# A reserve of MLP work after row 0, and a new interleaving of old steps with token steps, in a threshold-attention and MLP-mixer kernel

## The chip, the cores and the metric

The kernel runs on one core of one Trainium2 chip. The metric is the device time of one execution in microseconds (us); the number of a kernel is the median of several executions. A profiled execution gives the time of each instruction on each engine: PE (TensorE, matrix multiplication; its weight loads are listed apart as PEld), DVE (VectorE), ACT (ScalarE), POOL (GpSimd) and SP (SyncE, which here issues DMA transfers).

## The reference

Eight batch rows, eight heads, 576 positions, head dimension 64. The first block is attention with a threshold under the maximum; the second is a mixer MLP, along the positions (token MLP) and then along the features (channel MLP). The MLP weights come as 64-bit floats.

```python
scores = scale * np.matmul(q, k.transpose(0, 1, 3, 2))
thresh = np.max(scores, axis=-1, keepdims=True) - tau
scores = np.where(scores >= thresh, scores, -1000000000.0)
scores = scores - np.max(scores, axis=-1, keepdims=True)
attn = np.exp(scores)
attn = attn / (np.sum(attn, axis=-1, keepdims=True) + 1e-09)
x = np.matmul(attn, v)                       # (8, 8, 576, 64)
x = x.transpose(0, 2, 1, 3).reshape(8, 576, 512)
...
h = np.maximum(xt @ w_tok1, 0.0) @ w_tok2    # xt: x with its last two axes exchanged; 576 -> 256 -> 576
u = x + h.transpose(0, 2, 1)
h2 = np.maximum(u @ w_ch1, 0.0) @ w_ch2      # 512 -> 1536 -> 512
return u + h2
```

## The kernel before, in words

**Units.** Attention runs in 144 units, 18 for each batch row (`UB`, line 87). A unit is up to 128 query positions of two heads against all 576 keys; of nine units, the fifth (`SHARED`) takes the last 64 positions of two head pairs. The loop at line 525 has one iteration for each unit u, and some more at the end. It issues instructions for all engines in an order written out by hand; every engine works through its own queue in that order.

**One iteration.** `scores(u)`: PE multiplies (line 301), DVE takes the maximum of each of two heads (306), POOL makes the bias (307). The two score tiles in PSUM are the only two, so the next scores wait until ACT has read these. `norm(u-1)`: DVE's reciprocal (325, 326) and POOL's scaling (329). In rows 1 and later then `weight(2)`; `turn_blocks(u-2)`: DVE turns 32x32 blocks (363), and when a group of two units is complete, sixteen DMAs on the SP queue move the blocks to their places in eT (373). Then `fill(0.4)`, `weight(2)`, `weigh(u)`: ACT's Prelu (316) and Exp (319); `fill(0.6)`, `weight(2)`, the loads of q and k on the ACT queue (106) and of v on SP (114), and `prep`, which turns q and k on DVE (283). Last, `values` (403, 408) two iterations after its group was turned: PE multiplies eT by v, ACT copies the result into xT (413). In row 0 the turning is done on PE instead (352, 354).

**Weights.** `weight` decodes 31 pieces of the MLP weights from 64-bit to 32-bit floats, three steps to a piece, on ACT (191, 193), DVE (201, 205, 209) and POOL (215). The load of a piece (176) is on the SP queue and goes into one of four raw buffers, so it waits for POOL's last step of the piece four before. Row 0 does two steps in an iteration; from iteration 18 there are six, two pieces, and the last piece is done in iteration 27.

**MLP steps and their plan.** When the last values of row b are issued, `push(b)` puts the row's MLP into the list `todo`, as steps with a cost in planner's microseconds. The token steps, from `token_mlp`: five `turn_x` (PE transposes x, line 425; ACT copies it, 426; cost 0.44), two `tok1` (434, relu on ACT 435; cost 4.3) and eight `tok2` (441, DVE adds to xT, 445; cost 0.97). Each kind needs all of the kind before: tok1 all five turns, tok2 both tok1. The channel steps, from `channel_mlp`, for groups of 256 positions: twelve `ch1` (463, relu on ACT 464; cost 1.72, or 0.86 for the half group) and for each 128 positions four `ch2` (475, 479; 3.0 or 2.6), the last with DVE's copy (484) and a store on SP (485). tok1, tok2, ch1 and ch2 share a pool of two PSUM buffers, `ps_mm`.

`push` interleaves the token steps with what is left in `todo` from the row before (`old`), one by one, then appends channel groups 0 and 1 of the pair of rows (b even) or 2 to 4 (b odd). Then it sets a quota: the sum of all costs less `KEEP` (45, but 0 after row 0), over 17. `fill(share)` takes steps from the front while a credit, raised by share x quota, is above 0. push(0) comes at the end of iteration 20, push(1) at the end of 39, and each later one 18 iterations further, push(b) at the end of 18 b + 21. Row 2's units start with iteration 36.

The names below: scores(u) for the scores of iteration u, tok1(0), tok1(1) for the two tok1, "share" for one of the two `fill` calls of an iteration.

Of the kernel before, what the change touches and what calls it, by code (L numbers as in the profile page):

```python
# [21 lines left out]
def kernel(  # L22
# [35 lines left out]
    NT = NI + 1  # L58
    MT = [P] * NI + [LAST]
    NP = H // 2  # L60
    NTK = DTOK // P
# [25 lines left out]
    UB = 9 * NP // 2  # L87
# [328 lines left out]
    def token_mlp(b):  # L416
        xT = xTs.pop(b)
        o = S * (b % 2)
        s = {}

        def turn_x(t):
            M = MT[t]
            ps = ps_tr.tile([P, MAIN], F32, tag="tr", name=f"tx_{b}_{t}").rearrange("p (c x) -> p c x", c=NP)
            for p in range(NP):
                nc.tensor.transpose(out=ps[0:M, p, :], in_=xT[:, p, o + t * P : o + t * P + M], identity=ident)  # L425
            nc.scalar.copy(out=x_sb[0:M, t, :], in_=ps[0:M].rearrange("q p d -> q (p d)"))

        def tok1(m):
            need(2)
            if m == 0:  # L430
                s["a"] = work.tile([P, NTK, DM], F32, tag="a", bufs=1, name=f"a_{b}")
            ps = ps_mm.tile([P, DM], F32, tag="mm", name=f"t1_{b}_{m}")
            for t in range(NT):
                nc.tensor.matmul(ps, lhsT=w1[:, t, P * m : P * m + P], rhs=x_sb[:, t, :], start=(t == 0), stop=(t == NT - 1))  # L434
            nc.scalar.activation(out=s["a"][:, m, :], in_=ps, func=AF.Relu)

        def tok2(c, f):
            need(6)
            ps = ps_mm.tile([P, HS], F32, tag="mm", name=f"t2_{b}_{c}_{f}")
            for m in range(NTK):  # L440
                nc.tensor.matmul(  # L441
                    ps, lhsT=s["a"][:, m, P * c : P * c + P], rhs=w2[:, m, HS * f : HS * f + HS], start=(m == 0), stop=(m == NTK - 1)
                )
            u = xT[:, c, o + HS * f : o + HS * f + HS]
            nc.vector.tensor_add(out=u, in0=u, in1=ps)  # L445

        steps = [(0.44, lambda t=t: turn_x(t)) for t in range(NT)]
        steps += [(4.3, lambda m=m: tok1(m)) for m in range(NTK)]
        steps += [(0.97, lambda c=c, f=f: tok2(c, f)) for c in range(NCC) for f in range(2)]
        return steps  # L450
# [41 lines left out]


    KEEP = 45.0
    todo = deque()
    quota = 0.0
    credit = 0.0
# [11 lines left out]
    def push(b):  # L509
        nonlocal quota  # L510
        uT = xTs[b]
        steps, old = token_mlp(b), list(todo)
        todo.clear()
        for i in range(max(len(steps), len(old))):
            todo.extend(old[i : i + 1])
            todo.extend(steps[i : i + 1])
        for i in range(2) if b % 2 == 0 else range(2, (2 * S + GR - 1) // GR):
            todo.extend(channel_mlp(b - b % 2, uT, i))
        quota = (sum(c for c, _ in todo) - (KEEP if b else 0.0)) / (UB - 1)

    prep(0)
    due = deque()
# [2 lines left out]
    for u in range(len(units) + LAG + 4):  # L525
# [4 lines left out]
        if on:  # L530
            b_now, p0, t = units[u]
            n = b_now * NP + p0
# [8 lines left out]
        if back:  # L541
# [6 lines left out]
            if place == many - 1:  # L548
                b, p, c = key
# [24 lines left out]
        while due and due[0][0] <= u:  # L574
            _, b, p, c = due.popleft()
            values(b, p, c)
            if p == NP - 1 and c == 1:
                push(b)
    need(len(pieces) - 1)
    quota = 1e9  # L580
# [29 lines left out]
```

## Time and profile before

| what | value |
|---|---|
| median of 3 executions | 1402.13 us (1402.13 to 1402.17) |
| profiled execution, its own time | 1403.98 us |
| its span, first to last instruction | 1401.9 us |
| mean granted clock of PE | 0.986 of full |
| DMA | 128.34 MB, mean 92 GB/s |

The profiled execution in 40 equal slices of 35 us, each digit the busy share of a slice in tenths, 9 for 90% or more; PEclk is the granted clock of PE, in tenths:

```profile
PE   5776899989999999999999999999999999999998
ACT  5676564444545444453334444443334444220110
PEclk9998999989999999999999999999999999999999
```

Row 0, without MLP work, takes the first slices; row 1 starts at about slice 4, row 2 at about slice 8. The PE rows below are from the timeline: start and length of a run of instructions of one line in us, engine, line, operation, tiles, shape and count, and in brackets the idle time of the engine before it and what ended it. The lengths of matmuls are modelled, so two runs may overlap a little.

### The profile page before, as it was taken

To read this page: it belongs to the slowest core of one execution; us is meant where nothing else is said; L and a number is where in the kernel's file an instruction comes from. 1 tells how busy PE (TensorE), PEld (TensorE's weight loads), DVE (VectorE), ACT (ScalarE), POOL (GpSimd) and SP (SyncE) were. 2 spreads that over 40 slices of the span, in tenths; PEclk is the share of its full clock that TensorE was granted. 3 is DMA by queue.
4 is the path that set the end of the run, shared out by engine and by line. 5 is a ranking of instruction groups with operands and counts; after the bars stand their busy time and mean duration, and the time that the engine had idled before them with its cause. 6 is when DMAs were issued, how large, how long until landed. Compare 5 with 4: busy or idle time off the path is not lost.

```text
span 1401.9 us, 19510 instructions
## 1 busy us (share of the span) xinstructions
PE 1332.0 (95%) x6866; PEld 833.3 (59%) x6866; DVE 585.6 (42%) x1009; ACT 589.1 (42%) x1328; POOL 359.1 (26%) x683
## 2 busy tenths in 40 slices
PE   5776899989999999999999999999999999999998
PEld 3443566646665567565656566565657566576675
DVE  5689674445444443434333444434333444201000
ACT  5676564444545444453334444443334444220110
POOL 4466462222222222212122222222212222100000
PEclk9998999989999999999999999999999999999999
DMA  6344654443444444443334444343343433300000
GB/s 127 92 109 116 170 141 111 96 120 90 115 125 112 106 94 97 101 96 92 87 97 92 100 94 104 94 107 80 96 96 80 104 90 82 86 8 16 8 8 23
DMA packets 257376, 128.34 MB, mean 92 GB/s; under 512 B 208064, under 2 KB 221376, under 8 KB 257280
## 3 DMA queue, kind: packets, MB, share of 16 engines
q1 hardware_dynamic: 131632, 111.46, 30.3%
q10 hardware_dynamic: 125648, 15.64, 7.0%
q8 instruction: 55, 0.90, 0.3%
q14 instruction: 41, 0.34, 0.1%
HBM read 43.25 MB, written 9.44 MB: 38 GB/s over the span
## 4 chain that ended last, share of the span: by engine, by line
PE 83%; DVE 7%; SPq 3%; ACT 2%; DMA 2%; POOL 1%; issue 1%; DVEq 0%; ACTq 0%; POOLq 0%
PE c L479 27%; PE c L463 24%; PE sc L301 11%; PE pv L408 7%; PE t L434 4%; PE t L441 3%; DVE mx L306 3%; PE pv L403 2%; SPq L373 2%; DVE T L363 2%; PE tx L425 1%; PE c L475 1%; PE pv_s L408 1%; DMA scratch<-in_moe_w_ch_dram 1%; ACT e L316 1%
## 5 line engine op out<-in xcount | busy, mean ns | idle before, releaser
L306 DVE TENSOR_REDUCE mx<-sc 128x1 f32<-128x576 f32 x288 | 204.7, 752 | 530.6 <-PE sc L301 528.8
L463 PE MATMUL c<-xT,wc 128*128 128x256 f32 (+1 forms) x1920 | 401.7, 362 | 4.1 <-ACT g L464 2.0
L479 PE MATMUL c<-wc,g 128*128 128x512 f32 x864 | 388.9, 596 | 0.0
L463 PEld LDWEIGHTS c<-xT,wc 128*128 128x128 f32 x1920 | 332.8, 190 | 75.2 <-issue 27.2
L307 POOL TENSOR_SCALAR bias<-mx,toff 128x1 f32<-128x1 f32 x288 | 80.1, 278 | 824.0 <-DVE mx L306 768.1
L479 PEld LDWEIGHTS c<-wc,g 128*128 128x128 f32 x864 | 157.8, 190 | 177.8 <-issue 176.3
L316 ACT ACTIVATE e<-sc,bias 128x576 f32<-128x576 f32 x288 | 199.0, 740 | 145.5 <-POOL bias L307 142.9
L464 ACT ACTIVATE g<-c 128x256 f32<-128x256 f32 (+1 forms) x240 | 86.6, 363 | 347.9 <-PE c L463 332.5
L329 POOL TENSOR_SCALAR e<-e,rr 128x576 f32<-128x576 f32 x288 | 219.3, 774 | 16.2 <-DVE rr L326 4.0
L319 ACT ACTIVATE e<-e,ntau 128x576 f32<-128x576 f32 x288 | 220.2, 773 | 0.0
L301 PE MATMUL sc<-kT,qT 64*128 64x288 f32 (+1 forms) x1280 | 192.3, 439 | 18.6 <-ACT e L316 9.7
L363 DVE STREAM_TRANSPOSE T<-e 128x1152 f32<-128x1152 f32 x126 | 172.5, 1369 | 15.7 <-DMA eT<-T 8.4
L301 PEld LDWEIGHTS sc<-kT,qT 64*128 64x128 f32 (+1 forms) x1280 | 104.5, 181 | 95.8 <-issue 47.7
L408 PE MATMUL pv<-eT,lv 128*64 128x256 f32 x1024 | 127.0, 392 | 0.0
L408 PEld LDWEIGHTS pv<-eT,lv 128*64 128x64 f32 x1024 | 76.6, 142 | 40.0 <-issue 5.4
L413 ACT COPY xT<-pv 128x256 f32<-128x256 f32 x64 | 23.8, 372 | 172.2 <-PE pv L408 155.1
L484 DVE COPY o<-c 128x512 f32<-128x512 f32 x36 | 24.4, 678 | 164.6 <-PE c L479 164.6
L441 PE MATMUL t<-w,a 128*128 128x288 f32 x256 | 76.2, 426 | 12.2 <-DVE xT L445 10.1
L434 PE MATMUL t<-x_sb,w 128*128 128x512 f32 x160 | 73.4, 606 | 0.0
L441 PEld LDWEIGHTS t<-w,a 128*128 128x128 f32 x256 | 46.4, 194 | 35.9 <-DVE xT L445 15.2
L445 DVE TENSOR_TENSOR xT<-xT,t 128x288 f32<-128x288 f32 x64 | 28.0, 441 | 76.8 <-PE t L441 76.7
L319 ACT ACTIVATION_READ_ACCUMULATOR e<-e,ntau 128x1 f32 x288 | 57.1, 198 | 0.0
(48 smaller groups left out, 605.2 us busy)
## 6 DMA issues: line engine op xcount, KB each, us to landing
eT<-T SPq DMA_DIRECT2D x896, 72.0 KB, 2.1
scratch<-in_moe_w_ch_dram SPq DMA_DIRECT2D x24, 512.0 KB, 4.0
lv<-in_v_dram SPq DMA_DIRECT2D x32, 288.0 KB, 3.5
out_dram<-o SPq DMA_DIRECT2D x36, 256.0 KB, 2.2
eT<-T SPq DMA_DIRECT2D x224, 36.0 KB, 1.9
lk<-in_k_dram ACTq DMA_DIRECT2D x108, 72.0 KB, 2.8
lq<-in_q_dram ACTq DMA_DIRECT2D x104, 72.0 KB, 2.1
lq<-in_q_dram SPq DMA_DIRECT2D x24, 72.0 KB, 3.5
```

What stands on the lines that cost most here:

```text
L301: nc.tensor.matmul(sc[h][rows, f, 0:HS], lhsT=qT[r, cols], rhs=kT[r, HS * f : HS * f + HS], start=True, stop=True)
L306: nc.vector.tensor_reduce(out=mx[:, c], in_=sc[h][:, :, 0:HS], axis=AX.XY, op=ALU.max)
L316: nc.scalar.activation(out=eh, in_=sc[h][:, :, 0:HS], func=AF.Prelu, bias=bias[:, h : h + 1], scale=SCALE, alpha=STEEP)
L319: nc.scalar.activation(out=eh, in_=eh, func=AF.Exp, bias=ntau, accum_out=rs[:, h : h + 1])
L329: nc.gpsimd.tensor_scalar(out=eh, in0=eh, scalar1=rr[:, h : h + 1], scalar2=1.0, op0=ALU.mult, op1=ALU.mult)
L363: nc.vector.transpose(out=T.rearrange("p (a c n x) -> p c a n x", a=4, c=NK, n=n)[:, :, :, place, :], in_=e.rearrange("p (c a x) -> p c a ...
L408: nc.tensor.matmul(to[r], lhsT=lv[:, j, :], rhs=eT[:, j], start=False, stop=(c == NI - 1), skip_group_check=True)
L434: nc.tensor.matmul(ps, lhsT=w1[:, t, P * m : P * m + P], rhs=x_sb[:, t, :], start=(t == 0), stop=(t == NT - 1))
L441: nc.tensor.matmul(ps, lhsT=s["a"][:, m, P * c : P * c + P], rhs=w2[:, m, HS * f : HS * f + HS], start=(m == 0), stop=(m == NTK - 1))
L463: nc.tensor.matmul(ps, lhsT=wc1[:, j, c, :], rhs=uT[:, c, GR * i : GR * i + n], start=(c == 0), stop=(c == NCC - 1))
L464: nc.scalar.activation(out=s["g"][:, j, 0:n], in_=ps, func=AF.Relu)
L479: nc.tensor.matmul(flat, lhsT=s["g"][:, j, P * t : P * t + P], rhs=wc2[:, j, :], start=False, stop=(j == NJ - 1), skip_group_check=True)
```

## The change

After row 0, 20 of the planner's microseconds are taken out of the quota (`KEEP_FIRST`), as 45 are after the other rows. And `push` interleaves differently: one old step still goes ahead of each token step, but two go ahead of the first tok1 (index `NT` = 5) and of the first tok2 (index `NT + NTK` = 7). Old steps that are left follow the token steps. No instruction is added or taken away.

```diff
     KEEP = 45.0
+    KEEP_FIRST = 20.0
...
         steps, old = token_mlp(b), list(todo)
         todo.clear()
-        for i in range(max(len(steps), len(old))):
-            todo.extend(old[i : i + 1])
-            todo.extend(steps[i : i + 1])
+
+        for i, step in enumerate(steps):
+            n = 2 if i in (NT, NT + NTK) else 1
+            todo.extend(old[:n] + [step])
+            del old[:n]
+        todo.extend(old)
         for i in range(2) if b % 2 == 0 else range(2, (2 * S + GR - 1) // GR):
             todo.extend(channel_mlp(b - b % 2, uT, i))
-        quota = (sum(c for c, _ in todo) - (KEEP if b else 0.0)) / (UB - 1)
+        quota = (sum(c for c, _ in todo) - (KEEP if b else KEEP_FIRST)) / (UB - 1)
```

## The prediction

> **What bounds the kernel now.** I read the page first: its busy shares and the group of line 434, the first matmul group after the turned x.
>
> ```profile
> PE 1332.0 (95%) x6866; PEld 833.3 (59%) x6866; DVE 585.6 (42%) x1009; ACT 589.1 (42%) x1328; POOL 359.1 (26%) x683
> ...
> L434 PE MATMUL t<-x_sb,w 128*128 128x512 f32 x160 | 73.4, 606 | 0.0
> ```
>
> TensorE (PE) is busy 95% of the span, so moved work is worth something only where PE stands idle or runs at a lower clock. Line 434 (tok1) is preceded by 0.0 us of idle time in all its executions.
>
> Next, the timeline of PE, to find the holes (start, length, line, tiles, count, idle time and releaser). The first sits at the start of row 2, iterations 38 to 40 of the unit loop:
>
> ```profile
> 290.88 1.24 PE L301 MATMUL sc<-kT,qT 64*128 64x288 f32 x8
> 294.10 2.95 PE L301 MATMUL sc<-kT,qT 64*128 64x288 f32 x8 [1.98 <-ACT e L316]
> 299.18 1.12 PE L403 MATMUL pv<-eT,vl 128*64 128x256 f32 x4 [2.14 <-DMA eT<-T]
> 300.06 3.65 PE L408 MATMUL pv<-eT,lv 128*64 128x256 f32 x16
> 303.65 1.76 PE L301 MATMUL sc<-kT,qT 64*64 64x288 f32 x16
> 305.34 1.10 PE L425 MATMUL tx<-ident,xT 128*128 128x128 f32 x8
> ```
>
> There is no MLP group (lines 425 to 479) from 290.88 to 305.34: the list `todo` is empty. PE waits twice, and the eight score matmuls take 2.95 us in place of 1.24. The windows view gives the reason; its column behind POOL is the granted clock:
>
> ```profile
> 296.00:298.00 2.00, 1.04 (x4) 0.22 (x1) 2.00 (x4) 0.40 (x3) 0.27 (x1) 0.50 0.84 186
> 298.00:300.00 2.00, 0.82 (x4) 0.59 (x6) 1.60 (x4) 2.00 (x5) 1.71 (x4) 0.50 0.50 168
> ```
>
> The clock is halved after the gap of 1.98 us, and stays so until about 305.
>
> The other holes are in row 1, iterations 21 to 26:
>
> ```profile
> 137.61 6.15 PE L434 MATMUL t<-x_sb,w 128*128 128x512 f32 x10
> 145.63 1.82 PE L301 MATMUL sc<-kT,qT 64*64 64x288 f32 x16 [1.87 <-ACT e L316]
> ...
> 160.59 5.84 PE L441 MATMUL t<-w,a 128*128 128x288 f32 x16 [2.77 <-DVE xT L445]
> ...
> 192.73 3.72 PE L463 MATMUL c<-xT,wc 128*128 128x256 f32 x16 [2.05 <-ACT g L464]
> ```
>
> The last names ScalarE's relu, but ScalarE itself stood behind a decode of weights (lines 191 to 215), whose load stood behind sixteen issues on SP. Timelines of ACT and SP:
>
> ```profile
> 190.36 0.68 ACT L191 ACTIVATE scratch<-scratch 128x512 int32<-128x512 uint32 x1 [5.72 <-DMA scratch<-in_moe_w_ch_dram]
> ...
> 176.17 10.01 SPq L373 DMA_DIRECT2D eT<-T  x16
> 186.29 1.50 SPq L176 DMA_DIRECT2D scratch<-in_moe_w_ch_dram  x3
> ```
>
> From 420 us on, the view of waits has this for PE, and no more:
>
> ```profile
> PE t L441 <- DVE xT L445: 4.1, 6, 0.8
> PE t L441 <- ACT g L464: 1.8, 5, 0.4
> PE c L463 <- DVE xT L445: 1.7, 2, 0.8
> ```
>
> **The change, part by part.** No instruction is added or removed. The planner's sums give the order. In planner costs, push(0) holds 102.92; its quota falls from 102.92/17 = 6.05 to (102.92 - 20)/17 = 4.88 per iteration. From iteration 21 to 39 there are 19 shares: before, 17 of them empty the list at iteration 37; after, 95.1 is done by the end of 39 and 7.8 (three steps of 2.6) is left. PE takes 1.03 us for a unit of cost: twelve matmuls of line 479 for 5.2 take 5.35 us by the chain of waits.
>
> *1. Iterations 38 and 39 are filled: gain 8.7.* They get 5.2 and 5.6, about 5.4 and 5.8 us of PE. What ran from 290.88 to 305.34 (14.46 us) takes, start to start at full clock elsewhere: scores 1.17 (267.31 to 268.48), twice; one group of values 2.31 (288.57 to 290.88); the shared scores 1.13 (230.95 to 232.08); 5.78 in all. So 8.7 us are lost, 4.1 as waits and 4.6 by the clock. Does the new work cover them? Scores wait for the two Prelus of line 316, which end 3.8 us after the previous scores start (294.72); the next scores now start after 1.17 + 5.4. The values wait for eT until 299.18, 8.3 us after; they now come after 1.17 + 5.4 + 1.17 + 5.8 = 13.5. The eT issues (SP from 286.36) stand ahead of the moved steps, so they are no later. The moved channel steps carry two stores of 256 KB on SP from iterations 35 and 37 to 39 and 41, 0.53 us of issue each, behind the eT burst of their iteration. SP waits there for VectorE's copy (0.69 us), and a load of v or the next burst stands behind it, needed two iterations later; I put it at nothing. Without that cover the price would be one late eT, as above: 2.1 and a slow clock, 4.3.
>
> The Trainium skill has a rule here: "TensorE: Matmul & The Clock Gate", section "HAM oscillation — how this bites in real kernels", gives the abstract rule that the clock is safe while no idle gap of PE is over about 3.4 us. This trace disagrees: gaps of 1.98 and 2.77 us were each followed by a granted clock near a half. By the rule the hole would be worth only its waits, and the sum would end near 1399; the rows decide.
>
> *2. Row 1 gets less work per iteration: loss 0.9.* Through iteration 27 the planner does 44.7 before and 35.7 after: 9.0, or 9.3 us of PE, leave a stretch where the decode of two weight pieces per iteration goes on unchanged. I follow the order.
> - Before, tok1(0) and an empty second share in iteration 21 made scores(22) wait: Prelu stands behind relu(a) on ScalarE. 1.87, plus 0.65 as its second head waits (1.82 against 1.13 to 1.20). After, the five turns come alone, Prelu runs ahead of relu(a), and this wait is gone; but iteration 22 now has tok1(1) and an empty share, and no values behind it. The same 2.5 moves there.
> - tok2: with two PSUM buffers the third group in a row waits for the first add (line 445), which stands on VectorE behind two maxima, the reciprocal, decode and the transpose: 2.77 before, then 1.43 as 16 matmuls took 5.84 and not 4.41 at a clock of 0.6. After, iterations 23 and 24 have four tok2 each. From the end of scores to the end of the add: 1.42 + 0.33 + 0.41 + 0.70 + 1.37 + 0.44 = 4.7, less two tok2 of 1.1: 2.4, twice.
> - The 2.05 at 192.73: the eT bursts of iterations 23 and 24 (10 to 11 us on SP each) hold back the load that iteration 25 wants. My estimate, following each queue with the durations of these rows: the load is issued near 181 in place of 186.3, scores(26) come near 182.5 in place of 185.8, and with one channel group, not two, ahead of ScalarE's wait, 0.4 to 0.8 us of it reach PE.
>
> Before: 2.5 + 0.2 + 2.77 + 1.43 + 2.05 = 8.95. After: 2.5 + 2.4 + 2.4 + 0.8 = 8.1, and a half-clock window of 3.4 us after one of these gaps, worth 1.7: 9.8. Bounds: no such window, and SP's wait hidden, 7.3 (gain 1.6); three windows, 13.2 (loss 4.3); or all of the 9.3 turned into idle time (rival 1).
>
> *3. Row 2's token steps: 0.* push(1) has only three old steps. They go between the first turns and are used up before tok1, so "two older steps" finds none. Eight tok2 come as five and three after their scores; before, as four and four: two waits of 1.6 either way. One fewer or one more bounds it: 1.6 each way.
>
> *4. The new order in rows 3 to 8: 0.* Lists of 18 to 23 old steps come out at 19 to 23, and the reserves stay at 37 to 40. Two old steps ahead of tok1(0) cover the last turn's copy, ahead of tok2(0) the second relu. The first wait isn't there (0.0 above), the second neither (0.2 us, once, in row 1). The 7.6 us of row 3 and later come from two-buffer PSUM between alternating steps, which goes on in other phase. Bounds: all 7.6 gone, or as much again; nearest to no change, as the pattern is the same.
>
> **Sum.** 1402.13 - 8.7 + 0.9 = 1394.3. The profiled execution is 1403.98 with a span of 1401.9; its own sum is 1396.2, and the median stands 1.85 under it.
>
> **Rivals.**
> *Rival 1, the decode is the clock of row 1.* If the iterations up to the scores at 206.38 can't become shorter because SP's bursts, loads and ScalarE's decode set their pace, the 9.3 us taken out become idle time: 1402.13 - 8.7 + 9.3 = 1402.7, no change. For it: the 5.72 us wait of ScalarE, SP busy without a break from 161.88 to 187.8. Against: PE was busy 57.95 of the 60 us from 170 to 230, so it, not the decode, set most of them. Half of it gives 1398.1. Chance of the full case 0.10.
> *Rival 2, slower: the paired old steps.* Two old groups and then tok1 or tok2 make three users of a two-buffer PSUM pool in a row. If the third waits 2.05, as at 192.73, twice in each of six pushes, 24.6 us are added: 1394.3 + 24.6 = 1418.9. It decides from 7.8/12 = 0.65 us each. Against: three and more channel groups in a row run from 336 to 420 us with PE busy for 84.00 of 84 us. Chance 0.05.
> *Rival 3, row 1 calms too.* If half of its 8.95 goes, and some of the 7.6: 1402.13 - 8.7 - 4.5 - 1 = 1388. Chance 0.12.
> *Rival 4, the reserve never reaches the first units*, since 19 shares are spent on a quota for 17: then 1402. But 95.1 of 102.92 is a plain sum, and its last 10.8 fall in 38 and 39. Chance 0.02.
>
> **How the numbers follow.** The forecast has 0.71, with its own range from the bounds of parts 2 and 3: 1389.5 to 1399. Towards rival 1's half and rival 3 the range of 8 in 10 is 1388 to 1399.5. About 0.2%, 2.8 us, is what a measurement tells from no change, so faster means under 1399.3. Faster: the forecast's 0.71 less a tail of 0.03 above that, and rival 3: 0.80. Same: that tail, rivals 1 and 4: 0.15. Slower: rival 2, 0.05.
>
> **What would show it.** Right: groups of lines 463 and 479 between the scores of iterations 38 to 40, clock 1.00 there, no wait of pv for eT; scores(23), not scores(22), waiting for line 316; a wait for line 445 in both iterations 23 and 24; the idle time of row 1 between 7 and 13 us; that of row 3 and later near 7.6. Wrong: ScalarE waiting over 6 us for a weight load before 200 us with PE idle behind it (rival 1), or waits of over 0.65 us at tok1(0) or tok2(0) of each later row (rival 2).

## The result, and the profile after

| kernel | median, us | executions | ratio to the kernel before, 95% interval |
|---|---|---|---|
| before, beside it | 1401.74 | 6 | |
| changed | 1401.11 | 6 | 0.9997 (0.9985 to 1.001) |
| changed, a second round on another chip (before: 1402.15) | 1400.46 | 10 | 0.9992 (0.9981 to 1.0002) |

No difference that can be told: the forecast of 1394.3 and its range are missed. The profiled execution of the changed kernel took 1399.06 us with a span of 1397.3, 4.6 less than the one before; but its scores(21) start at 121.87 and not at 126.52, so all of this lies ahead of the first instruction that the change moves. From there to the end both take 1275.4.

The hole of iterations 38 and 39 is gone. Timeline of PE, changed kernel (start, length, line, tiles, shape, count, idle time and releaser):

```profile
269.07 1.24 PE L301 MATMUL sc<-kT,qT 64*128 64x288 f32 x8
270.24 5.42 PE L479 MATMUL c<-wc,g 128*128 128x512 f32 x12
275.58 1.24 PE L301 MATMUL sc<-kT,qT 64*128 64x288 f32 x8
276.75 2.84 PE L479 MATMUL c<-wc,g 128*128 128x512 f32 x6
...
282.54 0.65 PE L403 MATMUL pv<-eT,vl 128*64 128x256 f32 x4
```

Channel work stands behind each group of scores, no bracket names a wait, the scores take 1.24 and the values 0.65, where they took 2.95 and 1.12.

Row 1, the same view:

```profile
145.88 1.86 PE L301 MATMUL sc<-kT,qT 64*128 64x288 f32 x8 [1.88 <-ACT e L316]
...
152.36 3.79 PE L441 MATMUL t<-w,a 128*128 128x288 f32 x8 [2.48 <-DVE xT L445]
...
184.20 1.99 PE L463 MATMUL c<-xT,wc 128*128 128x256 f32 x8 [2.27 <-ACT g L464]
```

Scores(23), not scores(22), wait for Prelu, and tok2 waits in iteration 23 (152.36) and again in 24 (2.33 at 164.10), as forecast.

What was not forecast is in the view of waits from 420 us on:

```profile
PE t L441 <- ACT g L464: 6.6, 7, 2.3
...
PE t L434 <- ACT g L464: 0.7, 2, 0.4
```

tok2 (441) waits 6.6 us for relu of the channel groups in place of 1.8, with a longest wait of 2.3, and tok1 (434), which never waited, now does. The longest ones are in iterations 99 and 135. Timeline of PE and then of ACT in iteration 99, changed kernel:

```profile
796.86 1.24 PE L301 MATMUL sc<-kT,qT 64*128 64x288 f32 x8
798.03 2.05 PE L463 MATMUL c<-xT,wc 128*128 128x128 f32 x16
802.41 1.24 PE L441 MATMUL t<-w,a 128*128 128x288 f32 x4 [2.33 <-ACT g L464]
```

```profile
799.28 1.41 ACT L316 ACTIVATE e<-sc,bias 128x576 f32<-128x576 f32 x2 [2.09 <-POOL bias L307]
...
802.10 0.43 ACT L464 ACTIVATE g<-c 128x128 f32<-128x128 f32 x2
```

The first share of the iteration is empty. Its second share begins with the two old ch1 groups (x16) that the change put ahead of tok2(0). They fill both PSUM buffers in 2.05 us; their relus stand in ScalarE's queue behind Prelu and Exp of the same iteration and run only at 802.10. "PSUM — Partial Sum Buffer", section "Engine vs sequencer instructions", of the Trainium skill says that ScalarE's queue is strictly first in, first out; these rows agree.

In the kernel before, the first share of this iteration holds one old group, and PE waits 0.79 us. Timeline of PE, before:

```profile
809.16 1.05 PE L463 MATMUL c<-xT,wc 128*128 128x128 f32 x8
811.00 1.24 PE L441 MATMUL t<-w,a 128*128 128x288 f32 x4 [0.79 <-DVE xT L445]
```

**Where the time went.** To compare kernels that do different steps in an iteration, I take the stretch between two starts of scores in the timeline and subtract the PE time of the MLP steps that the plan puts there, at each step's pace in an unhindered part of the timeline (turn 0.54, tok1 4.45, tok2 1.08, ch1 1.78 or 0.90, ch2 2.67, the first of four 3.11). What is left is attention, waits and slow clock. For iterations 28 to 46, for example: 145.40 - 90.87 = 54.5 before, 138.45 - 93.10 = 45.4 after (the paces are given rounded here; with these the work comes out 0.1 higher).

| left over, us | 21 to 28 | 28 to 46 | 46 to 98 | 98 to the end |
|---|---|---|---|---|
| before, two profiles | 32.6, 35.5 | 54.5, 54.1 | 126.4, 126.4 | 116.0, 116.0 |
| changed, two profiles | 34.2, 33.7 | 45.4, 45.4 | 128.6, 128.5 | 121.5, 121.4 |
| reserve alone (e1) | 34.5 | 45.4 | 128.8 | 115.4 |
| interleaving alone (e2) | 34.5 | 53.9 | 125.4 | 122.0 |
| changed, no empty share (e3) | 34.6 | 45.9 | 127.5 | 116.7 |
| reserve alone, no empty share (e4) | 32.6 | 45.9 | 125.5 | 114.3 |
| pair ahead of tok1 only (e5) | 36.5 | 45.4 | 127.3 | 116.5 |
| pair ahead of tok2 only (e6) | 36.6 | 45.4 | 132.6 | 115.1 |
| reserve 45, no empty share (e8) | 45.4 | 45.0 | 128.1 | 115.2 |

The last three columns agree to 0.5 us between two profiles of one kernel, so differences of 1 us there mean something; in the first, the decode of weights, two profiles of the kernel before differ by 2.9. The changed kernel gains 9 from 28 to 46 and gives 2.1 and 5.4 back behind it.

The same subtraction on shorter stretches says where. Of the 5.4, iterations 98 to 102 (from 14.2 to 16.4) and 134 to 139 (from 15.4 to 17.5) cost 2.1 each at full clock; in each of the two profiles one of the two stretches is another 1.6 or 1.7 longer, at a slow clock (first and second profile: 45.13 and 46.73 us, 53.27 and 51.60); the rest gives 0.5 back. Of the 2.1, iterations 57 to 59 cost 1.1 and 63 to 67 cost 2.2, and the rest gives 1.2 back.

The 1.1 is a wait ahead of the values of iteration 59. It stands in all six profiles with the reserve and empty shares and in none without. The profile names no releaser, but the rows fit the same cause in the other PSUM pool, `ps_tr`, which also has two buffers. The second share, behind an empty first one, has two `turn_x`, and the values are the third user. ScalarE's copy of the first turn stands behind Prelu and Exp and ends at 439.20; the values start 0.10 later (timelines of ACT and PE, changed kernel). No run changes this wait alone.

```profile
438.63 0.57 ACT L426 COPY x_sb<-tx 128x512 f32<-128x512 f32 x1
```

```profile
439.30 0.65 PE L403 MATMUL pv<-eT,vl 128*64 128x256 f32 x4 [1.07 <-issue]
```

### The profile page after: what moved, and what is told of

Its sections match the earlier page's. It is cut to its first block, busy times and chain, and to the rows that moved or that the text cites. A ratio compares the mean times of both kernels' runs of the same rounds, so it can differ in the third digit from the quotient of the medians.

```text
span 1397.3 us, 19515 instructions
## 1 busy us (share of the span) xinstructions
PE 1325.4 (95%) x6866; PEld 831.1 (59%) x6866; DVE 585.5 (42%) x1009; ACT 588.0 (42%) x1328; POOL 356.5 (26%) x683
## 4 chain that ended last, share of the span: by engine, by line
PE 85%; DVE 7%; SPq 2%; DMA 2%; ACT 2%; issue 1%; POOL 1%; ACTq 0%; DVEq 0%; POOLq 0%
PE c L479 27%; PE c L463 25%; PE sc L301 11%; PE pv L408 7%; PE t L434 5%; PE t L441 3%; DVE mx L306 3%; PE pv L403 2%; SPq L373 2%; PE tx L425 1%; PE c L475 1%; PE pv_s L408 1%; DVE T L363 1%; DMA eT<-T 1%; ACT e L319 1%
## 5 line engine op out<-in xcount | busy, mean ns | idle before, releaser
L408 PE MATMUL pv<-eT,lv 128*64 128x256 f32 x1024 | 122.9, 382 | 0.0
L441 PE MATMUL t<-w,a 128*128 128x288 f32 x256 | 77.6, 432 | 16.4 <-DVE xT L445 9.8
```

What stands on the lines that cost most here:

```text
L408: nc.tensor.matmul(to[r], lhsT=lv[:, j, :], rhs=eT[:, j], start=False, stop=(c == NI - 1), skip_group_check=True)
L441: nc.tensor.matmul(ps, lhsT=s["a"][:, m, P * c : P * c + P], rhs=w2[:, m, HS * f : HS * f + HS], start=(m == 0), stop=(m == NTK - 1))
```

## The experiments

All are variants of the changed kernel but e7. e1 to e4 ran on one chip (before: 1402.20), e5 to e8 on another (1401.54), e9 and e10 on a third (1402.15).

**e1, the reserve alone.** The old order, since without pairs the new loop gives the same list.

```diff
-            n = 2 if i in (NT, NT + NTK) else 1
+            n = 1
```

> The reserve of 20 after row 0 alone; the interleaving is that of before (one old step ahead of each token step, no pairs). Theory P (the pairs give the gain back): iterations 38 and 39 are filled as in the changed kernel, row 1 loses about 2, and from row 3 on the waits of PE stay between 7 and 10 us in place of 13.7; the time is 5 to 7 us under the kernel before, near 1395. Rival Q (any shift of the left-over steps costs as much, pairs or not): the waits from row 3 on are near 13 and the time is within 2 us of before. Rival R (the gain is lost in row 1's decode): within 2 us of before, with the loss ahead of 210 us.

Measured 1395.25, ratio 0.9956 (0.9939 to 0.9973). The same 45.4 in the hole, and 115.4, no loss, from iteration 98 on. Theory P holds, Rival R falls. Rival Q holds for a part: from 46 to 98 the reserve alone stands at 128.8, 2.4 over the kernel before, with a wait of 1.68 us in iteration 63, one of 1.51 in iteration 66, where the left-over steps come in another phase, and the one of 1.07 in iteration 59. From 420 us on PE waits 10.8 us, a little over the 7 to 10 expected.

**e2, the interleaving alone.**

```diff
-    KEEP_FIRST = 20.0
+    KEEP_FIRST = 0.0
```

> The new interleaving alone, with its pairs; no reserve after row 0 (KEEP_FIRST 0). Theory P: the holes of iterations 38 and 39 stay, and waits for relu of 2.3 us stand ahead of tok2(0) in rows 4 and 6; from row 3 on PE waits for 11 to 14 us in place of 7.6, so 3 to 7 us over the kernel before, near 1406. Rival Q: about the same. Rival R: within 2 us of before.

Measured 1405.89, ratio 1.0032 (1.0021 to 1.0042): slower by itself, as expected, though PE waits 10.0 us from 420 us on where 11 to 14 were expected. The hole is back, and the same wait is in iteration 99. Timeline of PE, e2:

```profile
294.45 1.90 PE L301 MATMUL sc<-kT,qT 64*128 64x288 f32 x8 [1.98 <-ACT e L316]
...
811.21 1.24 PE L441 MATMUL t<-w,a 128*128 128x288 f32 x4 [2.33 <-ACT g L464]
```

The two parts of the change, at -0.44% (e1) and +0.32% (e2) beside the kernel before, sum to -0.12%; both together measured -0.03% and -0.08%. With intervals of 0.1 to 0.2% to each side, the parts add up as far as this can tell.

**e3, no empty share.** `fill` takes at least one step.

```diff
-        while todo and credit > 0:
+        first = True
+        while todo and (credit > 0 or first):
+            first = False
             cost, step = todo.popleft()
```

> The changed kernel, but each of the two shares of an iteration takes at least one step while there are any. Theory E (the pair costs only where the first share is empty, since the relus of the second share stand behind Prelu and Exp): iterations 99 and 135 then have one old group in the first share, the two waits of 2.3 us go to under 1, scores(23) no longer wait 1.9 for Prelu; 5 to 8 us under the changed kernel, near 1395. Rival T (two old groups and tok2 in a row wait wherever they stand): the waits stay above 2 and the time is within 2 us of the changed kernel.

Measured 1396.1, ratio 0.9963 (0.995 to 0.9976): by the ratios 4 to 5 us under the changed kernel, where 5 to 8 were expected. Iteration 99 in e3's timelines of PE and ACT:

```profile
798.53 2.05 PE L463 MATMUL c<-xT,wc 128*128 128x128 f32 x16
800.42 1.14 PE L441 MATMUL t<-w,a 128*128 128x288 f32 x4
802.34 1.16 PE L463 MATMUL c<-xT,wc 128*128 128x128 f32 x8 [0.79 <-DVE xT L445]
```

```profile
799.72 0.28 ACT L464 ACTIVATE g<-c 128x128 f32<-128x128 f32 x1 [2.04 <-PE c L463]
799.90 1.36 ACT L316 ACTIVATE e<-sc,bias 128x576 f32<-128x576 f32 x2
```

PE runs the same four groups in the same order. But the first now belongs to the first share, its relu is issued ahead of Prelu, and tok2 doesn't wait. Theory E holds: it is not three groups in a row that cost, but three whose first evictions (here the relus that free their PSUM buffers) stand behind `weigh`. In row 1 scores(23) no longer wait for Prelu, but tok2 in iteration 23 then waits 5.12 us in place of 2.48, so nothing is gained there (34.6).

**e4, the reserve without pairs, no empty share.** The edits of e1 and e3.

> The reserve without pairs, and at least one step in each share. Theories P and E together: 2 to 5 us under the kernel with the reserve alone, near 1392; iteration 63 and 79 lose their waits for the third group. Rival Q: no better than the changed kernel.

Measured 1392.33, ratio 0.993 (0.991 to 0.9949), 0.7% under the kernel before: the lowest ratio of the study, though its interval overlaps those of e1 and e5. The waits of the third group in iterations 63 and 79 (1.68 and 0.85 in e1) are gone, as expected.

**e5 and e6, one pair each.** `n = 2 if i == NT else 1`, and `n = 2 if i == NT + NTK else 1`.

> The changed kernel with two old steps ahead of the first tok1 only. The price of a share that follows an empty first share is counted from its first group: a relu of it is done 4.4 us on, an add 3.8 us on. In iterations 99 and 135 the second share has ch1, tok2, ch1, tok2: the third group can take the buffer of tok2, 3.8 - 2.0 = 1.8 us of wait in place of 2.3, and row 3's first push has no three groups behind an empty share. 4 to 6 us under the changed kernel, near 1396. If the pair ahead of tok1 were the dear one: no better than the changed kernel.

> The changed kernel with two old steps ahead of the first tok2 only. By the same price: iteration 63 has ch1, ch1, tok2 behind an empty share, half-size groups of 1.0 us, so 2.3 us of wait for relu; iterations 79 and 115 the same with full groups of 1.8, 0.8 to 0.9 us each; iterations 99 and 135 have an old group in the first share and wait under 1. 3 to 6 us under the changed kernel, near 1396. If any pair ahead of tok2 costs 2.3 or more: within 2 us of the changed kernel.

Measured 1394.17, 0.995 (0.9933 to 0.9967), and 1396.4, 0.9971 (0.9959 to 0.9983). The price worked out beforehand for a share behind an empty one held in e5 in iteration 99 (1.8 expected, first line, e5's timeline of PE) and in e6 in iteration 63 (2.3 expected, second line, e6's timeline); in iteration 79 it was 1.95, not 0.8 to 0.9 (third line, e6), and in iteration 115 it was 1.00:

```profile
804.28 1.16 PE L463 MATMUL c<-xT,wc 128*128 128x128 f32 x8 [1.68 <-DVE xT L445]
```

```profile
478.08 1.24 PE L441 MATMUL t<-w,a 128*128 128x288 f32 x4 [2.33 <-ACT g L464]
621.77 1.49 PE L441 MATMUL t<-w,a 128*128 128x288 f32 x4 [1.95 <-ACT g L464]
```

In iteration 79 of e6 a load of k (line 106) stands ahead of Prelu in ScalarE's queue and is issued only at 618.20; Prelu starts 2.46 us behind the start of the first old group, in iteration 115 only 1.51 behind it.

Each pair alone is cheaper than the two together: its place moves, and with it whether a first share is empty.

**e7, the kernel before again, and e10, the changed kernel again,** each for a second profile.

> The kernel before, unchanged, for a second profile of the same instructions. If the part of row 1 (iterations 21 to 28) differs by 1 to 3 us between two profiles of one kernel, the difference of about 2 us seen there between the changed kernel and the one before can't be told from none; if it agrees within 0.3 us, the reserve costs about 2 us there.

> The changed kernel again, beside the one above on the same chip, and a second profile of it: within 2 us of the kernel before; the waits of 2.3 us in iterations 99 and 135 are there again, and iterations 21 to 28 differ from the first profile by up to 3 us.

e7 was one execution of 1403.86. From 21 to 28 its left-over is 35.5 where the first profile of the same program has 32.6. Six profiles with the changed kernel's order in row 1 (changed twice, e1, e5, e6, e9) have 33.7 to 36.6, three with that of before (twice, e2) 32.6 to 35.5. So the reserve's loss in row 1 can't be told from none. e10 measured 1400.46, as in the table above; the waits of 2.33 are there again.

**e8, a reserve of 45.** e4 with `KEEP_FIRST = 45.0`.

> The reserve without pairs, at least one step in each share, and the reserve raised from 20 to 45. Row 1's MLP work through iteration 27 falls from 38 to 27 us of PE. If the decode of weights sets the pace of iterations 21 to 27 (some 8.5 us or more for each), PE gets most of these 11 us as idle time, and with the waits between tok2 gone (some 8 us in rows 1 and 2) the time is within 5 us of the kernel with the reserve of 20 and no empty shares. If the decode follows PE, scores(28) come 10 us earlier or more and the time falls by 6 to 8, near 1385.

Measured 1404.82, ratio 1.0022 (1.001 to 1.0033): by the ratios some 0.9% over e4, about 13 us, where the expectation with decode as the pace was within 5. Scores(28) come 72.7 us behind scores(21), where e4 needs 70.6 with 10.7 us more of MLP work in between: the decode sets the pace, and PE idles; a part is slow clock (0.81 granted in this stretch, 0.88 in e4). Timelines of SP, ACT and PE of e8 in iterations 25 and 26:

```profile
167.41 11.01 SPq L373 DMA_DIRECT2D eT<-T  x16
178.53 1.50 SPq L176 DMA_DIRECT2D scratch<-in_moe_w_ch_dram  x3
```

```profile
182.37 0.67 ACT L191 ACTIVATE scratch<-scratch 128x512 int32<-128x512 uint32 x1 [6.23 <-DMA scratch<-in_moe_w_ch_dram]
```

```profile
186.12 3.78 PE L463 MATMUL c<-xT,wc 128*128 128x256 f32 x8 [4.17 <-DVE xT L445]
```

A load of weights is issued behind sixteen eT issues, ScalarE waits 6.23 us for it and VectorE 1.83 (until 182.37), and PE stands 4.17 us for the add that VectorE does behind its share of the decode. That is rival 1 of the prediction, at a larger reserve: at 20 it costs one wait of 2.27 us, where the kernel before had 2.05, at 45 it sets the pace. The other half of the expectation, that 8 us come back because the waits between tok2 go, was wrong too: in row 1 the decode took the place of those waits, and from 28 to 46 e8 has 45.0, e4 45.9.

**e9, ScalarE's order in two iterations.** In iterations 99 and 135 alone, `weigh(u)` stands behind `fill(0.6)`.

```diff
-        if on:
+        swap = u in (99, 135)
+        if on and not swap:
             weigh(u)
         if b_now:
             fill(0.6)
+        if swap:
+            weigh(u)
```

> The changed kernel, but in iterations 99 and 135 alone weigh stands behind the second share on ScalarE, not ahead of it. If the 2.3 us ahead of tok2(0) there are the relus of the two old groups standing behind Prelu and Exp, both waits fall under 0.5; but Prelu then ends later and the next scores wait for it, some 1 to 2 us, so the time falls by 0 to 3 us. If the third group waits for something else (the adds, the loads, the weights), the waits of 2.3 stay.

Measured 1398.95, 0.9982 (0.9972 to 0.9992), 1.5 under the changed kernel beside it. Timeline of PE, e9, iteration 99:

```profile
798.50 2.05 PE L463 MATMUL c<-xT,wc 128*128 128x128 f32 x16
800.39 1.14 PE L441 MATMUL t<-w,a 128*128 128x288 f32 x4
...
803.41 1.86 PE L301 MATMUL sc<-kT,qT 64*128 64x288 f32 x8 [1.00 <-ACT e L316]
```

The wait ahead of tok2 is gone and a wait of 1.00 for Prelu stands ahead of the next scores: the order of ScalarE's queue is the cause of the wait, shown with nothing else changed. The gain in time is smaller than the waits: the ratio's interval meets that of the changed kernel, and in the profiles the stretch from scores(98) to the end is 2.2 us shorter. Of this 1.6 to 1.7 is that no slow clock follows; at full clock iterations 98 to 102 take 45.44 us, 45.13 in the changed kernel, and 134 to 139 take 50.70, before that 51.60.

## Why the prediction was wrong

- *Part 1, the hole, gain 8.7:* right in mechanism and size. The stretch from 28 to 46 gives 8.9 (54.3 to 45.4), with the slow clock gone and no late eT. The split into 4.1 of waits and 4.6 of clock holds for one execution only: in e7, the same program, the gap of 1.98 left the clock at 1.00, and the values then waited 3.15 for eT in place of 2.14, with a slow clock behind that; the left-over is the same (54.1).
- *Part 2, row 1, loss 0.9:* the waits moved as described. The last, put at 0.8, stayed at 2.27. In sum, the left-over from 21 to 28 has means of 34.0 before and 33.9 after (two profiles each): the loss isn't shown, and is within what one program does there from run to run. The sum of row 1 also left out its largest wait, ahead of the turns of iteration 21 (3.87 before, 3.76 after). It is in both kernels and cancels, but with it the idle time of row 1 is 14.4 (124 to 200 us), not the 7 to 13 named as a sign of being right.
- *Part 3, row 2, 0:* right. Two waits of tok2, 2.9 us together from 300 to 420, before 3.2.
- *Part 4, the new order in rows 3 to 8, 0: this step failed.* It cost 7.5 us (2.1 and 5.4 in the last columns), the upper bound that was given there ("as much again") and that I set aside with "the pattern is the same". The pattern was not the same. About 5 to 6 of it is the pairs (changed against e1: 121.5 against 115.4 from 98 on, level ahead of it); about 2 is the reserve itself (e1, 128.8 against 126.4), through the wait of 1.07 in iteration 59 and the other phase of row 3's steps.
- *Rival 2, chance 0.05, at 1418.9:* the right mechanism, wrongly dismissed and wrongly priced. I argued that from 336 to 420 us three and more channel groups run in a row without a wait. There the first share of such an iteration holds work, so the first relu is ahead of Prelu. The plan by itself shows where it is empty: in iterations 99 and 135 of the changed kernel, with three groups and more in the second. So not twelve places at 2.05, but two at 2.33, with a slow clock behind one of them.
- *Rival 1* is real, but only for a larger reserve (e8). That its 1402.7, and the 1402 of rival 4, lie near the measured 1401.11 is luck: the moved work filled iterations 38 and 39, and the gain went in rows 3 to 8.

The range failed with part 4: its bounds for that part were kept out of the range of 1388 to 1399.5, though 1394.3 + 7.6 = 1401.9 could be worked out from it. The forecast's own range of 1389.5 to 1399 is not quite its sum either: the bounds of parts 2 and 3 give 1390.2 to 1399.3.

## What to carry to other kernels

Work moved into a hole is worth the hole, but see what the list looks like behind it: write out, per share of each iteration, which steps the new plan puts there, and count the users of a small PSUM pool whose evictions stand behind a long block of the same iteration on the evicting engine. A pattern that runs free elsewhere proves nothing unless it stands at the same place in that engine's queue. Two parts of one change can cancel, so time each alone: here the reserve alone is 0.44% faster, the interleaving alone 0.32% slower, and neither shows in the sum.

## What the runs showed of the hardware

The same idle gap is not always followed by a slow clock. In the first profile of the changed kernel the gap of 2.33 us in iteration 99 left the clock at 1.00, while that of 2.33 in iteration 135 was followed by a granted clock near a half (windows view, the column behind POOL), and tok2 took 2.12 and not 1.24 us:

```profile
1128.00:1131.00 3.00, 3.00 (x10) 2.43 (x11) 0.45 (x1) 0.09 (x1) 0.00 (x0) 0.53 0.30 75
```

In the second profile of the same program it was the other way round: 0.73 behind iteration 99, 1.00 behind 135. The kernel before shows the same: the gaps of 1.98 and 2.77 us that the prediction read a slow clock behind are 1.98 and 2.78 in e7, with a granted clock of 1.00 behind each. A gap of some 2 us may thus cost 1.6 to 1.7 us more, or not, from one execution to the next. The rule of about 3.4 us that the prediction took from the Trainium skill ("TensorE: Matmul & The Clock Gate", section "HAM oscillation — how this bites in real kernels") does not cover this: all these gaps are shorter.
